# Attention with an adaptive layer norm and an MLP on one core: half cycles of three, three and two key tiles, and filling sums of 256 columns that share a bank

## The chip, the cores and the metric

One core of a Trainium2 chip runs the whole program. Its engines are TensorE (PE; its weight loads are listed apart as PEld), VectorE (DVE), ScalarE (ACT), GpSimd (POOL) and SyncE (SP, which here issues DMAs). The metric is device time in microseconds, the median over several executions. One execution was also profiled.

## The reference

An input x of 2048 rows and 512 columns goes through a transformer block whose layer norms are modulated by a condition vector c. The attention has 32 query heads of 16 columns and one key and one value head for all of them. The MLP is 1376 wide and its gelu is the tanh form.

```
mod = silu(c) @ w_mod                       # six rows of 512: sa, ca, ga, sb, cb, gb
h = layernorm(x) * (1 + ca) + sa
q, k, v = h @ wq, h @ wk, h @ wv            # q: 32 heads of 16; k and v: one head
p = softmax(q k^T / 4); o = p v
x = x + ga * (o @ wo)
h = layernorm(x) * (1 + cb) + sb
x = x + gb * (gelu(h @ w1 + b1) @ w2 + b2)
```

## The kernel before

**Units.** The 2048 rows are 8 blocks of 256 (`blocks`). A block has 8 units of 4 heads, so the loop at line 1350 goes through 64 units. In a unit, half s of the array (rows 0 to 63 or 64 to 127 of its contraction dimension) holds two heads j of 256 queries. There are 16 key tiles of 128 keys.

**What a unit does.** For each key tile and each half s a score product `e` (L607, 512 columns, 64 rows of the array) goes to one of three banks e0 to e2, and ScalarE writes its exponential to SBUF (L611, `p`). `pv` (L619, L628) multiplies the exponentials with the values: for each key tile four products of 32 array columns, which run at the same time and are listed as 8 instructions. The softmax's maximum is found ahead of time: 32 products `m` a unit (L505, 512 columns, 64 rows, tag `m` with three banks), each reduced by VectorE (`tensor_reduce`, L510). `put_max` (L529) takes the last maximum of a unit, turns it on VectorE and GpSimd and sends it by DMA into a row of the query tile, where the score product subtracts it. `lead` sets how far the maxima run ahead (32 a unit).

**Filling.** While one half of the array makes maxima and scores, the other works on a *batch* of other products, the filling: query projections of later blocks (`qproj_late`), and for each finished block its output projection, layer norm, transposes and MLP (`rest_steps`). A matrix product is three products of float32r parts (high and low). These jobs are Python generators in `queue`; `batches` (L167) cuts a sum into lists of products, `take` (L1169) fetches the next one, and `advance` goes on with the generator, which then also issues what reads the sum. A batch runs twice: rows 0 to 63 of its operands in one half cycle, rows 64 to 127 in the next, into the same bank, tag `x`. `half` (L187) lets the first product of a batch wait for the exponential of a score product (`state["witness"]`) that ran behind the other half's products, so that the two halves never write the bank at once.

**A cycle.** The loop at L1351 takes K and K+1, two pairs of key tiles X and Y: four cycles a unit. A cycle is:

1. `due()`, then a half cycle: half 1 gets n/2 = 4 maxima and 3 scores in turn (`mixture`, `beside`), half 0 the batch (6 products of 512 columns, or 12 of 256, `halves`) and a closing score (`follow`).
2. `end_step(*behind)`: the value products of the Y pair of the cycle before.
3. The other half cycle with the halves exchanged, the batch's second part in half 1, then what reads its sum.
4. `end_step(u, X)`: the value products of X.

`issue` (L1320) merges the two lists into program order: each entry has a length, and the list that stands earlier goes next. A maximum or score counts 1 and a product of a batch 0.75 for 512 columns (`AHEAD` / products), so that the batch stands somewhat ahead in program order. `beside` keeps the exponential of its last score back until the closing score's has been issued. Where the batch ends a sum, the reductions of the third and fourth maximum are issued behind what reads the sum (`hold`). Short batches (four products: the transposes, the last query groups) have an order of their own (`short`), and cycles without a batch another (`plain`), in which both halves share maxima and scores.

**Time in ticks.** `clock` counts four ticks a cycle, and `later(n, fn)` issues fn n ticks on (`due`). The DMAs that fetch a finished block's heads, the steps of the layer norm and of the gelu are placed so. For each of the 11 tiles of the first MLP `gelu` (L940) takes the sum out on VectorE with the bias (L949), squares it on ScalarE a tick later (L953), applies tanh four ticks later (L958), and GpSimd does the rest and splits the result into parts `gH` and `gL` six ticks later. The second MLP's sums are 512 columns wide, 33 products, and wait in Python until the gelu tiles they read have been issued (`made`).

**The end.** The last block's rest runs after the loop by itself on the whole array (`fast`), with what is left of the block before it (`tick`).

Of the kernel before, what the change touches and what calls it, by code (L numbers as in the profile page):

```python
# [32 lines left out]
BUSY = 5  # L33
BATCH = 6
SHORT = 4
LONG = (3, 1)
# [5 lines left out]
AHEAD = 4.5  # L42
# [8 lines left out]
def adaln_mqa_mlp(  # L51
# [127 lines left out]
    def whole(batch):  # L179
        for ps, a, b_, first_, last_ in batch:  # L180
            nc.tensor.matmul(ps, a, b_, start=first_, stop=last_)  # L181
# [5 lines left out]
    def half(one, s, behind=None):  # L187

        ps, a, b_, first_, last_ = one
        rows = slice(64 * s, 64 * s + 64)  # L190
        ins = nc.tensor.matmul(ps, a[rows], b_[rows], start=first_ and s == 0, stop=last_ and s == 1)  # L191
        if behind is not None:
            wait_for(ins, behind, "the other half of the array adds to the same bank")
# [254 lines left out]
    def qproj_late(b, g):  # L448
        ps = psum.tile([P, BQ], F32, name=f"qps{b}_{g}", tag="x")
        size_ = BATCH if (b, g) < LONG else SHORT  # L450
        yield from batches(ps, qpairs(b, g), size_)
        q32 = wts_pool["rest"].tile([P, BQ], F32, name=f"q32_{b}_{g}", tag="ot", bufs=2)
        if size_ == SHORT:
            nc.scalar.copy(q32, ps)
        else:
            nc.vector.tensor_copy(out=q32, in_=ps)
        qH, qL = qtiles(b, g)
        split(qH, qL, q32, nc.gpsimd, nc.gpsimd)
        later(4, lambda: send_q(b, g, qH, qL))
# [20 lines left out]
    class Max:  # L480
# [17 lines left out]
        def step(self, s, hold=None, **place):  # L498
# [4 lines left out]
            m = psum.tile([P, 512], F32, name=f"m{u}_{j}_{t}_{kc}_{s}", **(place or dict(tag="m", bufs=3)))  # L503
# [86 lines left out]
    def sexp(u, K, j, s, line=None):  # L590

        w = blocks[units[u][0]][1]
        qst = qsts[u]
        assert u in placed
        n = u * steps[0] + K
        if n < 3 and n not in pbufs:
            pbufs[n] = att.tile([P, 2, 2, 512], F32, name=f"p{n}", tag="p", bufs=3)
        pt = pbufs[n % 3]
        bank = banks.pop(0)
        banks.append(bank)  # L600
        e = psum.tile([P, 512], F32, name=f"e{u}_{K}_{j}_{s}", tag=f"e{bank}", bufs=1)
        rows = slice(64 * s, 64 * s + 64)
        if w == 512:
            kt, rhs = K, qst[rows, j, :]
        else:
            kt, rhs = 2 * K + j, qst[rows].rearrange("p j n -> p (j n)")
        nc.tensor.matmul(e, ks[rows, kt * P:(kt + 1) * P], rhs, start=True, stop=True)  # L607
        dst = pt[:, j, s, :]

        def exp():  # L610
            ins = nc.scalar.activation(dst, e, AF.Exp, scale=0.25)  # L611
            for old in written.pop((n - 3, j, s), ()):
                tc.declare_no_dep(ins.ins, old, reason="the products that read the tile's last contents come between the two")
            written.setdefault((n, j, s), []).append(ins.ins.name)
            return ins

        return exp() if line is None else line.append(exp)

    def pv(u, K):  # L619
        w = blocks[units[u][0]][1]  # L620
        if K == 0:
            accs[u] = psum.tile([P, w], F32, name=f"acc{u}", tag="v")
        pt = pbufs[(u * steps[0] + K) % 3]
        for kt in ([K] if w == 512 else [2 * K, 2 * K + 1]):
            for cidx in range(4):
                s, j = divmod(cidx, 2)
                rhs = pt[:, j, s, :] if w == 512 else pt[:, kt - 2 * K, s, j * w:(j + 1) * w]
                ins = nc.tensor.matmul(accs[u][32 * cidx:32 * cidx + 32, :], va[:, kt, :], rhs,  # L628
                                       start=kt == 0, stop=kt == NKT - 1)
                if kt % 2 and cidx:  # L630
                    wait_early(ins)

# [168 lines left out]
    def stir(starts):  # L801

        ps = psum.tile([P, BQ], F32, name=f"stir{len(idles)}", tag="x")
# [4 lines left out]
    def rest_steps(b, fast, rp, bank, ons, ready):  # L808
# [4 lines left out]
        for hf in range(w // HQ):  # L813
# [43 lines left out]
            pss = []  # L857
            for t in range(2):
                ps = psum.tile([P, D], F32, name=f"wops{b}_{hf}_{t}", **bank())
                pss.append(ps)  # L860
                if fast:
                    yield from batches(ps, out_pairs(t, range(KD - 1)), BATCH, end=False)
                    continue
                yield from batches(ps, out_pairs(t, range(KD)), BATCH)
                add_x(t, ps)

                for h in range(2):
                    later(3 - 2 * t + 2 * h, lambda t=t, h=h: stats(t, h))
            if fast:
# [10 lines left out]
            if not fast:  # L880
                later(4, lambda: rstd(0, 2))
                later(5, lambda: xhat(0))
                later(5, lambda: xhat(1))
                later(9, lambda: add_bias(0))
                later(9, lambda: add_bias(1))

                later(BUSY, lambda: state.update(busy=True))
                yield 8
# [3 lines left out]
            def modulate(dp, ps):  # L892
                if not fast:
                    src = rp.tile([P, 2, HQ], F32, name=f"tc{b}_{hf}_{dp}", tag="ot", bufs=2)
                    nc.scalar.copy(src, ps)
# [29 lines left out]
            else:  # L925
                for dp in range(KD // 2):
                    ps = psum.tile([P, 2, HQ], F32, name=f"tp2_{b}_{hf}_{dp}", **bank())
                    yield [(ps[:, d2, t * P:(t + 1) * P], xh[:, t, (2 * dp + d2) * P:(2 * dp + d2 + 1) * P], ident,
                            t + d2 == 0, t + d2 == 2) for t in range(2) for d2 in range(2)]
                    modulate(dp, ps)  # L930
                whole_h = clock[0] + 4
                state.update(busy=False, turns=2)
# [7 lines left out]
            def gelu(f, ps):  # L940
# [7 lines left out]
                else:  # L948
                    nc.vector.tensor_scalar(out=z, in0=ps, scalar1=b1c[:, f:f + 1], scalar2=None, op0=ALU.add)  # L949
# [20 lines left out]
                later(5 if fast else 6, last)  # L970
# [12 lines left out]
            for f in range(GROUP if fast else 0, NF):  # L983
# [3 lines left out]
                ps = psum.tile([P, HQ], F32, name=f"w1ps{b}_{hf}_{f}", **bank())  # L987
                pairs = [(w1t[:, 0, k, :], w1t[:, 1, k, :], hH[:, k, :], hL[:, k, :]) for k in range(KD)]
                if f or fast:
                    yield from batches(ps, pairs, 2 * BATCH)  # L990
                else:

                    yield from batches(ps, pairs, BATCH, lambda k: k < KD // 2 or clock[0] >= whole_h)
                if fast:
                    later(1, lambda f=f, ps=ps: gelu(f, ps))
                    yield 2
                else:
                    gelu(f, ps)
                    if f + 3 < NF:
                        later(1, lambda f=f: fetch_w1(b, w1ts, f + 3))  # L1000
            stage[b] = 1

            def store(t, ps, cols=slice(0, D)):
                row = row0 + hf * HQ + t * P
                ot = rp.tile([P, D], F32, name=f"ot{b}_{hf}_{t}", tag="ot", bufs=2)
                nc.vector.tensor_tensor(out=ot[:, cols], in0=ps[:, :cols.stop - cols.start], in1=x1[:, t, cols], op=ALU.add)
                send = lambda: nc.sync.dma_start(out=of[row:row + P, cols], in_=ot[:, cols])
                if fast:
                    send()
                else:  # L1010
                    later(2, send)
# [3 lines left out]
            for t in range(2):  # L1015
                sl = slice(t * P, (t + 1) * P)
                for cols in (slice(0, D), ):
                    place = dict(tag="m", bufs=3) if b == len(blocks) - 2 and t else bank()
                    ps = psum.tile([P, D], F32, name=f"w2ps{b}_{hf}_{t}_{cols.start}", **place)
# [480 lines left out]
```

## Time and profile before

| | us |
|---|---|
| median of 3 runs | 1565.02 (1564.38 to 1565.74) |
| profiled execution, first to last instruction | 1563.1 |
| TensorE busy | 1546.5 (99%) |
| VectorE busy | 1401.7 (90%) |
| ScalarE busy | 1228.8 (79%) |
| GpSimd busy | 681.7 (44%) |

The page gives the profiled execution by its span, the time from its first to its last instruction; the device times of the runs lie some 1.9 us above it. In the rows below, a line of the timeline has the start in us from the span's start, the length, the engine, the line of the code, the operation, what it writes and reads, and how many were merged into one row (their length then covers all). A bracket gives the engine's idle time before the row and what ended it. A line of a group has, behind the count, the busy time of all and the mean of one in ns, then the engine's idle time before them. A line of the windows has the stretch, its length, and for PE, PEld, DVE, ACT and POOL the busy us and the instruction count, then the clock, the share of DMA and GB/s. The granted clock was 1.00 throughout.

### The profile page before, as it was taken

Reading aid. Unit: us, or ns where it says so; the run is one execution under the profiler, and the core shown is the slowest. Engines: PE = TensorE matmul, PEld = TensorE weight load, DVE = VectorE, ACT = ScalarE, POOL = GpSimd, SP = SyncE. Lnnn points to the kernel's source line nnn. Section 1 sums busy time; section 2 is a strip of 40 time slices with the busy share of each in tenths; the row PEclk is TensorE's granted clock in tenths of the full one; section 3 lists DMA queues with packets and bytes.
Section 4 is the critical chain, followed back from the end, with each engine's and each line's share of the span. In section 5 each row is a group of like instructions: output and inputs, shape, how many; then the busy total and the mean of one; then the engine's idle time right before and its main releaser. Section 6 shows DMA issues by size and latency. Waiting matters only on the chain.

```text
span 1563.1 us, 41433 instructions
## 1 busy us (share of the span) xinstructions
PE 1546.5 (99%) x16387; PEld 959.9 (61%) x16387; DVE 1401.7 (90%) x2479; ACT 1228.8 (79%) x2392; POOL 681.7 (44%) x1194
## 2 busy tenths in 40 slices
PE   7999999999999999999999999999999999999999
PEld 4455555567655665557655675556655676556667
DVE  7999999999999999999999999999999999999625
ACT  5577778788777887788877887788877888788853
POOL 5545433877323570246422472245611573235711
PEclk9999999999999999999999999999999999999999
DMA  7235412313030211213022120303112130312241
GB/s 244 97 96 194 152 52 89 120 52 97 19 110 19 83 60 35 93 29 99 29 62 69 57 84 26 105 16 97 43 50 79 46 97 20 102 34 66 81 150 61
DMA packets 83126, 121.63 MB, mean 78 GB/s; under 512 B 19614, under 2 KB 56222, under 8 KB 82676
## 3 DMA queue, kind: packets, MB, share of 16 engines
q1 hardware_dynamic: 82916, 118.97, 23.5%
q8 instruction: 130, 2.13, 0.6%
q14 instruction: 64, 0.52, 0.1%
q10 hardware_dynamic: 16, 0.00, 0.0%
HBM read 91.13 MB, written 27.27 MB: 76 GB/s over the span
## 4 chain that ended last, share of the span: by engine, by line
PE 84%; DVE 10%; issue 3%; POOL 2%; DMA 1%; ACT 0%; ACTq 0%; SPq 0%; POOLq 0%; DVEq 0%
PE acc L628 28%; PE m L505 24%; PE e L607 16%; DVE mx L510 8%; PE w1ps L191 8%; PE w2ps L181 2%; PE w2ps L191 1%; PE w1ps L181 1%; DMA xt<-in_A_x_dram 1%; PE qps L191 1%; PE tp L191 1%; PE wops L191 1%; PE kps L162 1%; DVE st L835 1%; DVE x L828 1%
## 5 line engine op out<-in xcount | busy, mean ns | idle before, releaser
L510 DVE TENSOR_REDUCE mx<-m 128x1 f32<-128x512 f32 x2048 | 1270.5, 682 | 86.9 <-PE m L505 63.8
L611 ACT ACTIVATE p<-e 128x512 f32<-128x512 f32 x2048 | 1099.3, 598 | 257.4 <-PE e L607 110.5
L505 PE MATMUL m<-ks,qst 64*128 64x512 f32 x2048 | 832.4, 429 | 1.9 <-DVE mx L510 0.6
L607 PE MATMUL e<-qst,ks 64*128 64x512 f32 x2048 | 747.6, 412 | 0.1
L628 PE MATMUL acc<-p,va 128*32 128x256 f32 x8192 | 548.0, 385 | 0.0
L505 PEld LDWEIGHTS m<-ks,qst 64*128 64x128 f32 x2048 | 366.5, 184 | 212.3 <-DVE mx L510 174.8
L607 PEld LDWEIGHTS e<-qst,ks 64*128 64x128 f32 x2048 | 362.5, 184 | 95.2 <-ACT p L611 71.1
L628 PEld LDWEIGHTS acc<-p,va 128*32 128x32 f32 x8192 | 213.7, 109 | 213.1 <-issue 110.0
L553 POOL TENSOR_SCALAR mt<-turned 8x32 f32<-8x32 f32 x256 | 53.1, 208 | 418.9 <-DVE turned L559 406.9
L191 PE MATMUL w1ps<-h2H,w1t 64*128 64x256 f32 x1232 | 235.6, 287 | 0.0
L191 PEld LDWEIGHTS w1ps<-h2H,w1t 64*128 64x128 f32 x1232 | 185.8, 184 | 28.9 <-DVE mx L510 17.7
L191 PE MATMUL w1ps<-h2L,w1t 64*128 64x256 f32 x616 | 169.2, 275 | 0.0
L191 PE MATMUL w2ps<-w2H,gH 64*128 64x512 f32 x284 | 123.8, 436 | 0.0
L191 PEld LDWEIGHTS w1ps<-h2L,w1t 64*128 64x128 f32 x616 | 114.0, 185 | 0.0
L191 PE MATMUL w2ps<-w2L,gH 64*128 64x512 f32 x282 | 110.9, 393 | 0.0
L191 PE MATMUL w2ps<-w2H,gL 64*128 64x512 f32 x282 | 110.2, 391 | 0.0
L954 POOL TENSOR_SCALAR tt<-tt 128x256 f32<-128x256 f32 x77 | 31.0, 403 | 142.6 <-ACT tt L953 109.3
L137 POOL TENSOR_TENSOR gL<-z,gH 128x256 fp32r<-128x256 f32 x77 | 57.0, 740 | 6.4
L955 POOL TENSOR_TENSOR tt<-tt,z 128x256 f32<-128x256 f32 x77 | 56.7, 736 | 6.4
L965 POOL TENSOR_TENSOR z<-tt,z 128x256 f32<-128x256 f32 x77 | 56.4, 733 | 6.0
L964 POOL TENSOR_TENSOR tt<-tt,z 128x256 f32<-128x256 f32 x77 | 56.4, 732 | 0.0
L191 PEld LDWEIGHTS w2ps<-w2H,gL 64*128 64x128 f32 x282 | 52.2, 185 | 0.4
(190 smaller groups left out, 1480.9 us busy)
## 6 DMA issues: line engine op xcount, KB each, us to landing
w1t<-dw SPq DMA_DIRECT2D x82, 512.0 KB
qst<-dq SPq DMA_DIRECT2D x384, 32.0 KB
do<-oc SPq DMA_DIRECT2D x64, 128.0 KB
dw<-w1s SPq DMA_DIRECT2D x11, 512.0 KB
xt<-in_A_x_dram SPq DMA_DIRECT2D x4, 1024.0 KB
dq<-qH SPq DMA_DIRECT2D x16, 256.0 KB
dq<-qL SPq DMA_DIRECT2D x16, 256.0 KB
x<-in_A_x_dram SPq DMA_DIRECT2D x8, 512.0 KB
```

The lines of the kernel that those rows point to most:

```text
L137: eng_l.tensor_tensor(out=dst_l, in0=src, in1=raw(dst_h), op=ALU.subtract)
L181: nc.tensor.matmul(ps, a, b_, start=first_, stop=last_)
L191: ins = nc.tensor.matmul(ps, a[rows], b_[rows], start=first_ and s == 0, stop=last_ and s == 1)
L505: nc.tensor.matmul(m, qsts[u][rows, j, t * P:(t + 1) * P], ks[rows, kc * 512:(kc + 1) * 512], start=True, stop=True)
L510: nc.vector.tensor_reduce(out=self.mx[u][:, i, kc:kc + 1], in_=m, axis=AX.X, op=ALU.max)
L553: nc.gpsimd.tensor_scalar(out=mt[:, g:g + 32], in0=turned[g:g + 4 * T, :], scalar1=1.0, scalar2=0.0, op0=ALU.mult, op1=ALU.add)
L607: nc.tensor.matmul(e, ks[rows, kt * P:(kt + 1) * P], rhs, start=True, stop=True)
L611: ins = nc.scalar.activation(dst, e, AF.Exp, scale=0.25)
L628: ins = nc.tensor.matmul(accs[u][32 * cidx:32 * cidx + 32, :], va[:, kt, :], rhs, start=kt == 0, stop=kt == NKT - 1)
L955: nc.gpsimd.tensor_tensor(out=tt, in0=tt, in1=z, op=ALU.mult)
L964: nc.gpsimd.tensor_tensor(out=tt, in0=tt, in1=z, op=ALU.mult)
L965: nc.gpsimd.tensor_tensor(out=z, in0=tt, in1=z, op=ALU.add)
```

## The change

The loop takes three cycles a unit in place of four. `GROUPS` gives each cycle's key tiles X and Y: 3 and 3, 2 and 3, 3 and 2. The maxima are shared out by key tiles, so a cycle of six has 12 and one of five has 10. The exponentials' SBUF room, 12 tiles of 512 columns as before, is handed out tile by tile (`free`, `slots`) instead of by pairs.

The filling's bank is now one tile `fill` for the whole loop (tag `x`). Its sums are 256 columns wide and take its two halves in turn; only the transposes take it whole (`wide`). So the sums of the query projection, the output projection and the second MLP become two each. `compose` puts a batch together, up to 16, 16 and 14 units of 256 columns in the three cycles (two more where that ends a sum), across the ends of sums and jobs. What reads a sum waits for the batch's last product (`reads`), and the first product of the next batch waits for the readers as well as for the witness. Since the start of a sum marks the whole bank to be overwritten, only the first sum of an empty bank is started; one that follows beside a running sum finds its half zeroed by ScalarE (`finish`).

The first MLP's sums are taken out, with the bias, by ScalarE instead of VectorE. The query sums are copied by ScalarE, in two halves. The additions that take out the output projection and the second MLP stay on VectorE, now 256 columns each. Several steps are placed at other ticks: the gelu's last step five ticks on instead of six, the layer norm's steps two ticks nearer to each other. A tick is a quarter of a cycle as before, and there are 12 in a unit instead of 16. A finished block's job goes to the front of the queue instead of its end. `short` is gone, and `AHEAD` 0.75 says the same share for a product as before.

```
-BUSY = 5
+BUSY = 3
-SHORT = 4
-LONG = (3, 1)
+GROUPS = ((3, 3), (2, 3), (3, 2))
+UNITS = (16, 16, 14)
+SPILL = 2
-AHEAD = 4.5
+AHEAD = 0.75
...
+        def place(self):
+            return fill["bank"] if self.wide else fill["bank"][:, 256 * self.where:256 * self.where + 256]
...
+    def reads(ins):
+        if fill["last"] is not None:
+            wait_for(ins, fill["last"], "the filling's bank is being written")
+        fill["reads"].append(ins)
+        return ins
...
-                    nc.vector.tensor_scalar(out=z, in0=ps, scalar1=b1c[:, f:f + 1], scalar2=None, op0=ALU.add)
+                    reads(nc.scalar.activation(z, ps, AF.Identity, bias=b1c[:, f:f + 1]))
...
-                later(5 if fast else 6, last)
+                later(5, last)
...
+    def compose(cap):
+        batch, ends, used = [], [], 0
+        while True:
+            if not pulled:
+                op = pull()
+                if op is None:
+                    break
+                pulled.append(op)
+            one, n = pulled[0]
+            left = sum(units_of(b_) for _, _, b_ in one.ops[n:])
+            if n == 0:
+                where = (0, 1) if one.wide else (fill["next"],)
+                if any(fill["unread"][r] for r in where) or used and used + SPILL >= cap:
+                    break
+                begin = not any(fill["flight"])
...
+            if used + units_of(one.ops[n][2]) > cap + (SPILL if used + left <= cap + SPILL else 0):
+                break
...
+        return batch, ends, used / 2
+
+    def finish(ends, ins):
+        fill["last"] = ins
+        for one in ends:
+            one.done(one)
...
+        for one in ends:
+            if not one.wide and fill["flight"][1 - one.where]:
+                fill["reads"].append(nc.scalar.copy(one.place(), zeros.to_broadcast([P, HQ])))
+                fill["zero"][one.where] = True
...
-        for K in range(0, steps[u], 2):
-            goal = lead[u] + (lead[u + 1] - lead[u]) * (K + 2) / steps[u]
+        kt = 0
+        for (nx, ny), room in zip(GROUPS, UNITS):
+            X, Y = list(range(kt, kt + nx)), list(range(kt + nx, kt + nx + ny))
+            kt += nx + ny
+            goal = lead[u] + (lead[u + 1] - lead[u]) * kt / NKT
...
-            batch = take() if behind else None
...
+            batch, ends, long = compose(room) if behind else ([], [], 0)
+            if batch:
+                k = min(max(1, round((n / 2 + nx + ny - long) / 2)), nx + ny - 1)
+                which = X + Y
+                groups = [mixture(maxes(1, n // 2, 0.01), beside(1, which[:-k])),
+                          exps(0, which[:k - 1]) + halves(batch, 0) + [(1.0, lambda: follow(0, which[k - 1]))]]
+                issue(*groups)
...
+                issue(mixture(maxes(0, n // 2, 0.01, hold), beside(0, which[k:])),
+                      exps(1, which[-k:-1]) + halves(batch, 1) + [(0.0, go_on), (1.0, lambda: follow(1, which[-1]))])
```

372 lines of the change are left out of this document (212 added, 160 removed).

## The prediction

> **What bounds the kernel now.** I read the page first (busy shares, the chain, the costliest groups), then the timeline of a few half cycles, then the groups and windows of the engines that the change loads.
>
> ```profile
> span 1563.1 us, 41433 instructions
> PE 1546.5 (99%) x16387; PEld 959.9 (61%) x16387; DVE 1401.7 (90%) x2479; ACT 1228.8 (79%) x2392; POOL 681.7 (44%) x1194
> PE 84%; DVE 10%; issue 3%; POOL 2%; DMA 1%; ACT 0%; ACTq 0%; SPq 0%; POOLq 0%; DVEq 0%
> L510 DVE TENSOR_REDUCE mx<-m 128x1 f32<-128x512 f32 x2048 | 1270.5, 682 | 86.9 <-PE m L505 63.8
> L611 ACT ACTIVATE p<-e 128x512 f32<-128x512 f32 x2048 | 1099.3, 598 | 257.4 <-PE e L607 110.5
> ```
>
> TensorE is busy 99% and carries 84% of the chain, but VectorE is at 90%: the second bound is close. The loop of 64 units has this frame:
>
> ```profile
> 79.59 0.49 PE L191 MATMUL qps<-h0H,wqH 64*128 64x512 f32 x1
> ...
> 1508.25 1.93 PE L628 MATMUL acc<-p,va 128*32 128x256 f32 x32
> ...
> 1510.11 0.50 PE L181 MATMUL wops<-woH,onH 128*128 128x512 f32 x1
> ```
>
> From 79.59 to 1510.11 the loop takes 1430.5 us: 510 of its 512 half cycles, 2.80 each. One full half cycle, array and VectorE:
>
> ```profile
> 999.91 0.49 PE L505 MATMUL m<-ks,qst 64*128 64x512 f32 x1
> 1000.25 0.39 PE L607 MATMUL e<-qst,ks 64*128 64x512 f32 x1
> 1000.44 2.48 DVE L510 TENSOR_REDUCE mx<-m 128x1 f32<-128x512 f32 x4 [0.36 <-PE m L505]
> 1000.48 0.39 PE L505 MATMUL m<-ks,qst 64*128 64x512 f32 x1
> ...
> 1001.41 0.41 PE L505 MATMUL m<-ks,qst 64*128 64x512 f32 x1
> ...
> 1001.75 1.07 PE L628 MATMUL acc<-p,va 128*32 128x256 f32 x16
> 1002.75 0.49 PE L505 MATMUL m<-ks,qst 64*128 64x512 f32 x1
> ```
>
> Seven 512-column products stand behind each other on each half of the array. I call such a place a slot. The second starts 0.34 after the first, the seventh at 1.50, so a slot is (1.50-0.34)/5 = 0.23 us. The value products begin 0.34 after the last slot's start, and the next half cycle 1.00 after that. A half cycle is 0.34 + 0.23 x (slots-2) + 0.34 + values, here 2.84. The values of two key tiles cost 1.00; the row at 1508.25 has four, and 1.86 pass until 1510.11, so a tile is 0.43 and the change of tiling costs 1.00-0.86 = 0.14, beside the 0.34 at either end of the slots. That is what fewer half cycles can save.
>
> **Part 1: six half cycles in place of eight.** A unit keeps its 64 half-array products for maxima and scores, its 16 value tiles (16 x 0.43 = 6.88) and nearly its filling: 16+16+14 = 46 pieces of 256 columns against 4 x 12 = 48. The code gives a half cycle 6 maxima and 4 scores beside 1 score, 16 pieces and 1 score (ten slots each) where it has three tiles on both sides; where five tiles are split in two, 5 maxima and 3 or 4 scores, and nine slots. By the array alone: ten slots 0.34+8x0.23+0.34 = 2.54 (with 0.232), nine 2.30; values 2 x 1.00 + 4 x 1.43 = 7.72. Unit: 2 x 2.54 + 4 x 2.30 + 7.72 = 22.0, against 8 x 2.84 = 22.7. The switching saved, 0.7 a unit, would be 46 us over 64 units.
>
> But the maxima have three banks, as before, and now come six in a row instead of four. The first reduction starts 0.53 behind its product (999.91 to 1000.44); four take 2.48, so they follow at (2.48-0.68)/3 = 0.60. The sixth product needs the third reduction's bank: 0.53 + 2x0.60 + 0.68 = 2.41. What such a wait looks like stands in a half cycle without filling:
>
> ```profile
> 1032.92 6.66 DVE L510 TENSOR_REDUCE mx<-m 128x1 f32<-128x512 f32 x11
> ...
> 1033.60 0.50 PE L607 MATMUL e<-qst,ks 64*128 64x512 f32 x2
> ...
> 1034.85 0.18 PEld L505 LDWEIGHTS m<-ks,qst 64*128 64x128 f32 x1 [0.41 <-DVE mx L510]
> ...
> 1035.28 1.07 PE L628 MATMUL acc<-p,va 128*32 128x256 f32 x16
> 1036.28 0.19 PEld L607 LDWEIGHTS e<-qst,ks 64*128 64x128 f32 x2 [0.41 <-ACT p L611]
> ```
>
> The third of the eleven reductions ends at 1032.92 + 2x0.598 + 0.68 = 1034.80; the waiting weights load at 1034.85, and the value products begin 0.43 later. So in the ten-slot half cycles the values begin at 2.41+0.05+0.43 = 2.89, not 2.54. With five maxima it is the second reduction: 1.81+0.05+0.43 = 2.29, level with the array's 2.30. In the kernel before it was the first: 1.21+0.48 = 1.69, inside 1.84. The six half cycles are 2.89+1.00, 2.89+1.43, 2.30+1.43, 2.30+1.00 and twice 2.30+1.43: 22.70 a unit. VectorE takes back 45 of the 46 us.
>
> A thinner batch does not shorten these, since maxima set them; only a cycle with no filling does.
>
> ```profile
> L181 PE MATMUL w2ps<-w2H,gL 128*128 128x512 f32 x35 | 13.9, 396 | 0.0
> ```
>
> The queue holds 14 query groups of 24 pieces and 7 blocks of 328 (48 output projection, 16 transposes, 132 and 132), less what is left for the end: now 35 products in each of three forms run there on the whole array, 22 of them the last block's, so about 38 in all of the block before it, or 76 pieces. 336+2296-76 = 2556 pieces of 64 x 46 = 2944. Some 25 of 192 cycles stay empty. An empty half cycle now lasts 2.68 (1033.60 to 1036.28), 0.16 under a full one; with the score banks as its limit I take 0.2: 25 x 2 x 0.2 = 10 us. Loop after: 64 x 22.70 - 10 = 1443; before, with the two half cycles left out, 1430.5+5.7 = 1436. Term: **+7**.
>
> **Part 2: sums of 256 columns.** Twice the weight loads and products for the same columns. The first MLP has them already:
>
> ```profile
> 1072.11 0.38 PE L191 MATMUL w1ps<-h2H,w1t 64*128 64x256 f32 x1
> 1072.33 0.28 PE L191 MATMUL w1ps<-h2H,w1t 64*128 64x256 f32 x1
> 1072.44 0.39 PE L607 MATMUL e<-qst,ks 64*128 64x512 f32 x1
> 1072.45 0.27 PE L191 MATMUL w1ps<-h2L,w1t 64*128 64x256 f32 x1
> 1072.56 0.27 PE L191 MATMUL w1ps<-h2H,w1t 64*128 64x256 f32 x1
> ...
> 1074.95 0.18 PEld L505 LDWEIGHTS m<-ks,qst 64*128 64x128 f32 x1 [0.41 <-DVE mx L510]
> ```
>
> One each 0.115, half a slot, and the half cycle is 2.84 as with 512. Price nothing; the loads hide behind the other piece's streaming.
>
> **Part 3: ScalarE takes the first MLP's sums, and clears banks.** A sum that ends while its neighbour runs is zeroed by a ScalarE copy.
>
> ```profile
> 675.00:1075.00 400.00, 399.79 (x4496) 249.98 (x4496) 375.45 (x655) 328.59 (x644) 169.54 (x316) 1.00 0.19 60
> L949 DVE TENSOR_SCALAR z<-w1ps,b1c 128x256 f32<-128x256 f32 x77 | 37.1, 482 | 3.8 <-PE w1ps L191 3.5 <-PE m L505 0.3
> L945 ACT ACTIVATE z<-w1ps,b1c 128x256 f32<-128x256 f32 x11 | 5.2, 474 | 3.0 <-PE w1ps L181 3.0
> L640 ACT COPY oc<-acc 128x256 f32<-128x256 f32 x64 | 23.8, 372 | 5.8 <-PE acc L628 5.6
> L953 ACT ACTIVATE tt<-z 128x256 f32<-128x256 f32 x77 | 32.4, 421 | 0.0
> 1044.94 2.06 ACT L611 ACTIVATE p<-e 128x512 f32<-128x512 f32 x4 [0.15 <-PE e L607]
> ```
>
> VectorE loses 77 x 0.48 = 37 us, worth nothing on the path where 2.84 did not contain it. ScalarE gains, for each sum, 0.47 (L945) and 0.37 for the clearing (no such row; the nearest, the 256-column copy of L640). In the first MLP's stage, 77 x 12/46 = 20 units, 3.83 sums a unit come with two gelu steps of 0.42: 3.83 x 1.68 = 6.4 us beside 32 exponentials. Back to back these follow at (2.06-0.60)/3 = 0.49, 15.7 in all, so 22.1 of 22.7. Lower bound of the cost: 0, since that fits. Upper: with the exponentials at the row's 1099.3/64 = 17.2, 6.4+17.2+0.4 = 24.0, 1.3 a unit, 26 us. I worked through the shortest half cycle (2.30+1.00 = 3.30): first exponential at about 0.77, five of them 2.45, then 1.33 sums' worth of evacuation, clearing and square, 1.33 x 1.27 = 1.7 by durations, about 1.3 back to back: done at 4.5 to 4.9, where the next half's first exponential could start at 3.30+0.53 = 3.83. The fourth score waits for that exponential's bank, so 0.55 to 1.1 a unit are lost, one half cycle in six. I take 0.6 x 20 = **+12**.
>
> **Part 4: VectorE's evacuations.** The second MLP's and output projection's additions become twice as many at about 0.48 (L949, the nearest 256-column row). One in the 3.30 us half cycle, behind five reductions (0.53+3.00), ends at 4.0 where the next reduction could start at 3.83, and more with the unit's final maximum. Between 0 (absorbed) and 0.5 for the third of 56 sums that fall there, 9 us; I take **+5**. Late GpSimd products for the second MLP, whose first sum now runs in two cycles: 0 to 3 us a block, 0 to 21; I take 0, since the gelu steps were also moved a tick earlier. The end keeps its left-over work: 0, plus or minus 8.
>
> **Sum.** 1563.1 + 7 + 12 + 5 = 1587.1; the runs lie 1.9 above the profiled span (1565.02 in the median), so **1589 us**.
>
> **Rivals.** *The array is the bound after all* (faster): if the maxima's reductions keep ahead, the ten-slot half cycles start their values at 2.54, and 128 x 0.35 = 45 us come off. With ScalarE and VectorE hidden too: 1565 + 7 - 45 + 5 (empty cycles save less) = 1532. For it: in full half cycles VectorE now never holds the array. Against: 2.41 follows from two rows. It decides at a stall of 0.30 per ten-slot half cycle if nothing else costs, at 0.16 if all the other terms hold.
>
> *Strict order on the array.* The filling stands ahead of its place in program order (0.375 for half a slot), so the closing score is issued before the last two scores or maxima of the other half. If a product cannot start before an earlier one, five-tile half cycles of 0 + 16 + 1 (two a unit) last a slot longer: 0.23 x 2 x 64 x 0.87 = 26 us, 1615. Against: the piece at 1072.33 starts ahead of the score at 1072.44, which the code issues before it. The Trainium skill's page "TensorE: Matmul & The Clock Gate", section "The mechanism", states the strict form (starts and ends in program order); by that rule the sum would be 1615, and the trace disagrees by one place at least.
>
> *ScalarE or GpSimd sets the first MLP's stage:* the upper ends, 26+21 in place of 12: 1624.
>
> *The cycles even out:* empty cycles and fewer switches cancel the new waits, 1565.
>
> **How the numbers follow.** The forecast (1570 to 1605) 0.45; strict order or its like 0.12; ScalarE or GpSimd 0.14; the array's bound, wholly or partly, 0.24; even 0.05. The range leaves out the lower half of the faster cases and the end of the slow ones: 1545 to 1630. Runs of this kernel differ by 0.1%, so 0.2%, 3 us, is about what can be told from no change. Faster 0.24, same 0.05, slower 0.71.
>
> **What would show it.** In the trace after: value products of 24 starting 2.89 behind the half cycle's start where there are six maxima, with a weights load of m waiting for VectorE; 2.30 at five; pieces of 256 at 0.115; ScalarE nearly without idle time in the first MLP. Wrong if ten-slot half cycles take 2.54, or if first-half filling waits for clearing copies everywhere.

## The result, and the profile after

The changed kernel takes 1755.26 us in the median (1752.56 to 1768.16) where the kernel before, run beside it, takes 1564.78: a ratio of 1.123, with an interval of 1.120 to 1.127. Slower was forecast, but at 1589 us, and the time lies far outside the range to 1630.

The page after, first its span, busy times and chain, then the two costliest groups:

```profile
span 1753.6 us, 44436 instructions
...
PE 1641.2 (94%) x17936; PEld 1125.2 (64%) x17936; DVE 1380.2 (79%) x2419; ACT 1271.5 (73%) x2564; POOL 682.5 (39%) x1194
...
PE 84%; ACT 5%; DVE 5%; SPq 2%; DMA 2%; issue 1%; POOL 1%; DVEq 0%; POOLq 0%
...
L547 DVE TENSOR_REDUCE mx<-m 128x1 f32<-128x512 f32 x2016 | 1259.0, 684 | 278.9 <-PE m L542 156.9
L647 ACT ACTIVATE p<-e 128x512 f32<-128x512 f32 x2048 | 1087.6, 600 | 358.6 <-PE e L644 323.8
```

TensorE is no longer the bound throughout: 94% in place of 99%, so 112 us of its span are idle (16.6 before). Its share of the chain is 84% as before; ScalarE has 5% of it (0 before) and VectorE 5% (10 before). Yet no engine has become full instead: VectorE fell from 90 to 79%. It waited 278.9 us ahead of its reductions (86.9 before), ScalarE 358.6 ahead of the exponentials (257.4). Engines that wait for each other suggest a problem of order, which the page alone does not show.

Windows of the loop, of the end, and of short stretches in which the array waits (the columns as in the section on the profile before):

```profile
85.00:1693.00 1608.00, 1517.52 (x17282) 1041.35 (x17278) 1283.92 (x2216) 1207.43 (x2440) 631.55 (x1118) 0.97 0.20 64
1693.00:1753.00 60.00, 52.05 (x330) 45.61 (x323) 27.45 (x71) 15.95 (x41) 5.33 (x6) 0.97 0.26 97
488.60:500.50 11.90, 6.69 (x48) 4.70 (x44) 3.93 (x6) 3.48 (x6) 3.96 (x3) 0.71 0.05 12
493.07:499.90 6.83, 5.60 (x35) 4.41 (x39) 2.63 (x4) 2.98 (x6) 0.00 (x0) 0.50 0.00 1
544.27:547.68 3.41, 2.16 (x20) 1.00 (x20) 3.41 (x9) 2.69 (x6) 2.32 (x3) 1.00 0.00 0
549.10:556.20 7.10, 6.28 (x40) 2.58 (x38) 3.77 (x6) 3.65 (x7) 3.84 (x3) 0.50 0.18 50
```

The loop lasts 1608 us in place of 1430.5, which is +178 of the +190.5 between the two profiled spans. The start is 5 us longer and the end 7. The last four rows show something that the loop before has nowhere: stretches in which the array is granted half of its clock. The 0.71 of the third row is a mean: from 493.07 to 499.90 the clock was 0.50.

Three kinds of half cycle show where the loop's time is. The first is one that begins a unit, once in each block (start us, length, engine, line, operation):

```profile
478.99 0.44 POOL L138 TENSOR_TENSOR ml<-mt,mh 8x128 fp32r<-8x128 f32 x1
...
481.82 0.33 SPq L780 DMA_DIRECT2D drs<-rsum  x1
...
483.29 2.47 SPq L797 DMA_DIRECT2D os<-drs  x4
...
485.85 1.88 SPq L513 DMA_DIRECT2D qst<-dq  x3
...
491.24 0.67 SPq L585 DMA_DIRECT2D qst<-mh  x1
...
493.80 0.76 PE L644 MATMUL e<-qst,ks 64*128 64x512 f32 x1 [4.71 <-DMA qst<-ml]
```

The parts of the unit's maximum row are ready on GpSimd at 479.43. SyncE's queue sends them from 491.24 only: ahead of them stand a finished block's factors on their way to DRAM and back (L780, L797) and the next query tile (L513). The score that reads the row waits 4.71 us, and the pieces behind it then run at 0.50 of the clock. The half cycle takes 11.9 us instead of 3.9. Seven of them come to 9.9 to 11.9.

The second is the ordinary half cycle of nine slots, 16 pieces and values of three tiles, which starts at 707.35:

```profile
709.22 0.27 PE L193 MATMUL fill<-w2H,gL 64*128 64x256 f32 x1
709.25 0.50 PE L644 MATMUL e<-qst,ks 64*128 64x512 f32 x2
709.59 0.39 PE L542 MATMUL m<-ks,qst 64*128 64x512 f32 x1
709.91 1.50 PE L662 MATMUL acc<-p,va 128*32 128x256 f32 x24
```

The last piece starts at 709.22, 1.87 behind the start, as the array allows. But a score and the last maximum of the *other* half of the array start only then: the score at 709.25, beside the closing score (709.33; they share one row), and the maximum another 0.34 later. The values begin at 2.56 where 2.30 was forecast. The median over 79 such half cycles is 3.99 (forecast 3.73), and 3.56 over the 39 with values of two tiles (3.30). The ten-slot ones have 4.04 and 4.39 (3.89 and 4.32), those of nine slots with 14 pieces 3.75 (3.73).

The third has no filling:

```profile
343.51 0.50 PE L644 MATMUL e<-qst,ks 64*128 64x512 f32 x2
...
344.69 0.50 PE L644 MATMUL e<-qst,ks 64*128 64x512 f32 x1 [0.45 <-ACT p L647]
...
346.60 0.49 PE L542 MATMUL m<-ks,qst 64*128 64x512 f32 x1 [0.80 <-DVE mx L547]
...
347.03 1.07 PE L662 MATMUL acc<-p,va 128*32 128x256 f32 x16
```

A score waits for an exponential, a maximum for a reduction, and the values begin 3.52 behind the start. The loop has 30 of this kind: 24 last from 4.5 to 7.1 us and six, which have fewer maxima, 3.0 to 3.6, where I had taken them to be 0.2 shorter than the full ones.

### The profile page after: what moved, and what is told of

Same layout as the page of the kernel before. It is cut to its first block, busy times and chain, and to the rows that moved or that the text cites. A ratio compares the mean times of both kernels' runs of the same rounds, so it can differ in the third digit from the quotient of the medians.

```text
span 1753.6 us, 44436 instructions
## 1 busy us (share of the span) xinstructions
PE 1641.2 (94%) x17936; PEld 1125.2 (64%) x17936; DVE 1380.2 (79%) x2419; ACT 1271.5 (73%) x2564; POOL 682.5 (39%) x1194
## 4 chain that ended last, share of the span: by engine, by line
PE 84%; ACT 5%; DVE 5%; SPq 2%; DMA 2%; issue 1%; POOL 1%; DVEq 0%; POOLq 0%
PE acc L662 27%; PE m L542 20%; PE fill L193 18%; PE e L644 15%; DVE mx L547 4%; ACT p L647 3%; SPq L585 1%; DMA qst<-ml 1%; PE w2ps L182 1%; PE w1ps L182 1%; DMA xt<-in_A_x_dram 1%; SPq L513 1%; PE fill L182 1%; PE kps L163 1%; ACT tt L1005 0%
## 5 line engine op out<-in xcount | busy, mean ns | idle before, releaser
L547 DVE TENSOR_REDUCE mx<-m 128x1 f32<-128x512 f32 x2016 | 1259.0, 684 | 278.9 <-PE m L542 156.9
L647 ACT ACTIVATE p<-e 128x512 f32<-128x512 f32 x2048 | 1087.6, 600 | 358.6 <-PE e L644 323.8
L193 PE MATMUL fill<-h2H,w1t 64*128 64x256 f32 x1232 | 233.6, 284 | 0.0
L193 PEld LDWEIGHTS fill<-h2H,w1t 64*128 64x128 f32 x1232 | 190.0, 186 | 0.1
L193 PE MATMUL fill<-h2L,w1t 64*128 64x256 f32 x616 | 173.1, 281 | 0.0
L193 PE MATMUL fill<-w2H,gH 64*128 64x256 f32 x560 | 164.0, 293 | 0.0
L193 PE MATMUL fill<-w2H,gL 64*128 64x256 f32 x560 | 162.4, 290 | 0.0
L193 PE MATMUL fill<-w2L,gH 64*128 64x256 f32 x558 | 158.4, 284 | 0.0
L193 PEld LDWEIGHTS fill<-h2L,w1t 64*128 64x128 f32 x616 | 114.7, 186 | 0.2 <-ACT p L647 0.2
L193 PEld LDWEIGHTS fill<-w2H,gL 64*128 64x128 f32 x560 | 107.4, 192 | 0.4
L193 PEld LDWEIGHTS fill<-w2H,gH 64*128 64x128 f32 x560 | 107.5, 192 | 0.0
L193 PEld LDWEIGHTS fill<-w2L,gH 64*128 64x128 f32 x558 | 106.8, 191 | 0.0
```

The costliest lines, as they stand in the source:

```text
L547: nc.vector.tensor_reduce(out=self.mx[u][:, i, kc:kc + 1], in_=m, axis=AX.X, op=ALU.max)
L647: ins = nc.scalar.activation(slot(i), e, AF.Exp, scale=0.25)
```

## The experiments

Half cycles are named below by their slots and pieces; lengths are medians, counted from one start to the next. Every time stands beside the kernel before on the same chip (1564.0 to 1566.0).

### The late row, and the filling's lead

```
-MAX_WAIT = (1, 4)
+MAX_WAIT = (1, 2)
```

> The changed kernel with the four transfers of a unit's maximum row issued two ticks after the maximum instead of four, so that they stand ahead of the next query loads on SyncE's queue. Late-row theory: once a block the first half cycle of a unit stands 7 us because these transfers wait behind 4 + 8 others; with them ahead, eight stalls of about 7 us go, 57 us in all: 1755 to about 1698, and the granted clock comes back from 0.97 to near 1.00. Rival (the stall is the query load itself or GpSimd, and the row is only what the profile names last): less than 10 us.

1718.7 us (two executions, 1714.5 and 1722.9): 36.5 less than the changed kernel, not 57. The changed kernel's list of waits (us in total, times, longest) has this line, and this run's has not:

```profile
PE e L644 <- DMA qst<-ml: 41.2, 20, 4.7
```

At least part of the missing 20 us moved to the next transfer in the same queue. From this run's list:

```profile
PE m L542 <- DMA qst<-dz: 11.4, 7, 2.7
```

Maxima now wait for the next query tile, 11.4 us in 7 times. The half cycles that begin a unit still reach 5.2 to 7.0.

```
-AHEAD = 0.75
+AHEAD = 1.0
```

> The changed kernel with AHEAD 1.0 instead of 0.75, so that a filling piece counts its full half slot in the merge and the closing score stands behind the other half's products in program order. Order theory: the nine-slot half cycles lose their extra 0.24 us, 203 of them, 47 us: 1755 to about 1708; the value products begin 2.30 to 2.35 behind the half cycle's start instead of 2.56. Rival (ScalarE's clearing copies delay the witness, and with it the pieces): no more than 10 us either way, and 2.56 stays.

1776.8 us: 21 *more*. The 16-piece half cycles of nine slots did get shorter, by 0.13, but those of 14 pieces went from 3.75 to 4.10, because a piece now stands behind a score that waits. The expectation took the lead for a cost alone; it also protects the pieces.

> Both edits. If the two theories hold and do not share their time: 57 + 47 = 104 us, 1755 to about 1651. What then stays above the kernel before (1565) would be the maxima's three banks (ten-slot half cycles 2.89 instead of 2.54), the half cycles without filling or with little, and the ends. If one frees time that the other eats: 1680 to 1700.

1726.4 us (1722.4 to 1730.4), far from 1651, and no better than the early row alone.

### The same lead in the kernel before

```
-AHEAD = 4.5
+AHEAD = 6.0
```

> The kernel before with the filling standing at its own place in program order (AHEAD 6.0 for six products in place of 4.5), so that the closing score is issued behind the other half's last product and no piece ahead of its time. If the array's program order binds products of one half behind waiting products of the other, a piece now stands behind a score or maximum that waits for its bank: half cycles of 2.84 grow by 0.1 to 0.3, +50 to +130 us over some 430 of them. If the order does not matter: 1565, within 3.

1580.8 us, ratio 1.0097 (1.0082 to 1.0112). So the program's order on TensorE is worth time in the kernel before too, but less than expected: mainly the 138 half cycles of the first MLP grew, by 0.08 in the mean, and those of six 512-column products kept their 2.84.

### Do the reductions hold the array?

```
-  in_=m, axis=AX.X, op=ALU.max
+  in_=m[:, 0:256], axis=AX.X, op=ALU.max
```

> Both edits, and each reduction of a maximum reads 256 of its 512 columns (and the exponential's scale is made small so that nothing overflows): the output is not the reference's, since half of each maximum and the softmax's scale are left out; instructions and their order stay. Bank theory: the third of six reductions then ends by about 1.8 instead of 2.41, so ten-slot half cycles begin their values at 2.54 instead of 2.89 or later: 94 x 0.36 = 34 us or a little more under the run with both edits. Rival (the array's slots or ScalarE's exponentials set these half cycles): under 10 us.

1657.7 us, 69 less than with both edits above. That looked like VectorE as the cause, in twice the size expected. The control:

> The kernel before, whose reductions read 256 of the 512 columns (half of each maximum left out, and the softmax's scale changed so that the exponentials stay finite). The control for the halved reductions. If the full half cycles before are bound by the array, as predicted (2.84), these stay at 2.84 and only the half cycles without filling (2.68 each) can shorten: 1565, at the least 1535. If VectorE set part of the time before as it does after (-69 us there), about 1500.

1553.4 us: 12 us less. The full half cycles stayed at 2.84 and only thin ones changed (2.71 to 2.65), so the kernel before is bound by its array, as the prediction had it.

### The filling by itself, and ScalarE's part

```
-GROUPS = ((3, 3), (2, 3), (3, 2))
-UNITS = (16, 16, 14)
+GROUPS = ((2, 2), (2, 2), (2, 2), (2, 2))
+UNITS = (12, 12, 12, 12)
```

> The changed kernel with the key tiles shared out as before (four cycles of 2 and 2, 12 units of filling each); sums of 256 columns, batches across sums, the clearing copies and ScalarE's evacuations all stay. Theory (the half cycles of five and six tiles, and what a unit of 12 ticks does to the maximum row, carry the loss): about 1565, within 20. Rival (the filling's bank, its clearing copies and ScalarE carry a large part): 1620 or more.

1605.8 us, ratio 1.026 (1.025 to 1.028), between the two. So about 150 us belong to the new half cycles, with what their fewer ticks do to SyncE's queue, and about 41 to the new filling. Its trace shows ScalarE in the first MLP, and what starts the next half cycle's filling:

```profile
550.77 0.48 ACT L996 ACTIVATE z<-fill,b1c 128x256 f32<-128x256 f32 x1
...
551.28 0.38 ACT L1285 COPY fill<-mm 128x256 f32<-128x256 f32 x1
551.59 1.08 ACT L647 ACTIVATE p<-e 128x512 f32<-128x512 f32 x2
...
551.88 0.18 PEld L542 LDWEIGHTS m<-ks,qst 64*128 64x128 f32 x1 [0.41 <-DVE mx L547]
...
552.24 0.18 PEld L193 LDWEIGHTS fill<-h2H,w1t 64*128 64x128 f32 x1 [0.17 <-ACT p L647]
```

The evacuation (`z`) and the clearing copy stand ahead of two exponentials. The half cycle starts at 551.88, but its first piece at 552.24, when an exponential of the half cycle before is done. That half cycle takes 3.15 us; some 90 are between 3.1 and 3.35.

> The kernel before with one line changed: the first MLP's sums go out through ScalarE. Step of the prediction: ScalarE's work in that stage, without clearing copies, is 3.83 x (0.47 + 2 x 0.42) = 5.0 us beside 15.7 of 22.7 us a unit, so it fits: 0 to +5, and less idle time of ScalarE there. Rival (ScalarE's place in the order of a half cycle costs, as in the 3.30 us half cycle of the prediction): +10 to +26.

1565.4 us, ratio 1.000 (0.999 to 1.001): the evacuation through ScalarE costs nothing by itself.

```
-  fill["reads"].append(nc.scalar.copy(one.place(), zeros...))
+  fill["reads"].append(nc.vector.tensor_copy(out=one.place(), in_=zeros...))
```

> The previous kernel with the old half cycles and the new filling (1605.8), whose 91 clearing copies of the filling's bank go through VectorE in place of ScalarE. Its trace has 90 half cycles of the first MLP at 3.15 in place of 2.85: the copy (0.38) stands on ScalarE ahead of the exponentials, so the closing score's exponential comes late and the next batch's first piece waits for it. If that is the cause: 90 x 0.30 = 27 us less, 1579. Rival (the evacuation through ScalarE alone, or the wait for the readers, is what holds the batch): 1600 or more.

1605.9 us: no change, and my expectation fell. VectorE's rows of the same place:

```profile
551.63 0.43 DVE L1285 COPY fill<-mm 128x256 f32<-128x256 f32 x1 [0.42 <-ACT z L996]
551.97 3.67 DVE L547 TENSOR_REDUCE mx<-m 128x1 f32<-128x512 f32 x6
```

Here the copy waits for `z` and the next half cycle's reductions wait behind the copy. The pieces start with the half cycle, and the maxima are late instead.

> The kernel with the old half cycles and the new filling (1605.8), without the 91 clearing copies (so sums that start beside a running one add to the old content: the clearing is left out). If the copy lies on the path on either engine: 1575 to 1580, the 90 half cycles of 3.15 back at 2.85. If the batches across sums or the 256-column evacuations are what costs: 1600 or more.

1584.3 us: without the copies 21.5 us are gone, so the copy lay on the path on either engine. It explains about half of the 41. The other 20 stay open; 15 half cycles of 3.3 to 3.5 and 28 more full batches than before are part of them.

> The changed kernel with the maximum row sent two ticks earlier (1718.7 alone), and the 70 clearing copies through VectorE. In these half cycles of nine and ten slots VectorE sets the values' start and the batch's first piece mostly starts with the half cycle, so ScalarE's copies lie beside other work: 0 to -8, 1711 to 1719. If the copies cost here what they do in half cycles of two tiles: -21, 1698. If VectorE's 0.3 us each lengthen its chain: +10 or more.

1712.9 us, but from 1705.7 to 1720.0, against 1718.7: unclear. Nor does this run price the copies here: with the old half cycles the same move to VectorE changed nothing either, while leaving the copies out was worth 21.5 us. The changed kernel was not run without them.

### The rest of the queue

```
-  nc.sync.dma_start(out=drs[b]..., in_=rsum)
+  nc.gpsimd.dma_start(out=drs[b]..., in_=rsum)
-  nc.sync.dma_start(out=oss[hf][:, 1, g, :], in_=src)
+  nc.gpsimd.dma_start(out=oss[hf][:, 1, g, :], in_=src)
```

> The changed kernel with the maximum row sent two ticks earlier (1718.7), and a finished block's softmax factors (their way to DRAM and back, L780 and L797) issued from GpSimd's queue in place of SyncE's. Theory (SyncE's queue stands still behind these transfers, and the next query tile, issued behind them, comes late: the eight half cycles that begin a unit at 5.2 to 7.0 us): these fall to about 4.1, 15 to 20 us less, about 1700. Rival (the transfers are late for another reason, or GpSimd, waiting for the round trip, is late with its own steps): within 5 of 1718, or slower.

1701.9 us (1700.0 to 1704.7), as expected: 16.8 less than the early row alone, whose two executions lie 8 us apart. The maxima's wait for the query tile fell to one of 3.2 us:

```profile
PE m L542 <- DMA qst<-dz: 3.2, 1, 3.2
```

One half cycle that begins a unit stays at 9.0, the last block's.

### The order on the array

```
+  a = 1.0 if nx + ny == 5 and len(batch) == 16 else AHEAD
```

> The changed kernel with the maximum row sent two ticks earlier (1718.7), and the filling no longer ahead in program order only where five maxima stand beside 16 pieces. Order theory: these 118 half cycles fall from 4.00 and 3.56 by the 0.13 that the run without any lead showed, while the others keep their lengths: 15 us less, about 1703. If that run's 0.13 came from its other half cycles' lengths: no change.

1713.9 us, 5 less than the 1718.7 and not 15, which is within the spread of that run's two executions. The 118 half cycles did fall by the 0.13 in the median, to 3.86 and 3.42, and summed over both profiles they are 11 us shorter. Those of 14 pieces took 8 of it back (3.77 to 3.98 in the mean): 13 of them have a score that waits for ScalarE's exponential. Of the 38 with ten slots and values of two, 12 rose from 4.04 to about 4.37, but their sum grew by less than 2.

> The changed kernel with the maximum row sent early and the factors on GpSimd's queue (1701.9), whose reductions read 256 of the 512 columns (half of each maximum left out, and the softmax's scale changed so that the exponentials stay finite). If VectorE's reductions carry the rest: the half cycles fall to the array's lengths, 3.54 and 3.97 with ten slots and 3.30 and 3.73 with nine: 1560 to 1590. If the array's order carries as much: nine slots stay near 3.8 and ten near 3.9 and 4.2, about 1635.

1665.4 us, above both expected cases. The full half cycles with 16 pieces did not move at all: 3.99, 3.56, 4.04 and 4.56, the same as in the run with whole reductions. A nine-slot one of this kernel, which starts at 504.22:

```profile
506.10 0.28 PE L193 MATMUL fill<-woH,onL 64*128 64x256 f32 x1
506.13 0.49 PE L644 MATMUL e<-qst,ks 64*128 64x512 f32 x2
506.46 0.38 PE L542 MATMUL m<-ks,qst 64*128 64x512 f32 x1
506.78 1.50 PE L662 MATMUL acc<-p,va 128*32 128x256 f32 x24
```

The last piece, the two scores and the maximum stand as they did in the changed kernel. What the 36 us came from is mostly half cycles without filling (4.96 to 4.43; 22 us) and others with little. So neither VectorE nor the maxima's banks set the length of the full half cycles. The program's order is what is left. This is the end of a ten-slot half cycle in the changed kernel's list of TensorE's instructions, in program order:

```
L193 fill
L193 fill
L644 e33_1_0      the closing score, behind the last piece on its half
L542 m35_0_0_0    \ two maxima of the other half,
L542 m35_0_0_1    / issued behind the closing score
L662 acc ...
```

The list says how many come behind the closing score: with 16 pieces at 0.375 it stands at 6.0 in nine slots and at 7.0 in ten, and the other half's last two products at 6.01 and 7.01, or 7.01 and 8.01 (the first maximum counts 0.01). With 14 pieces none comes behind it, with 18 one, and in the kernel before one (4.5 against 5.01). Among those of 14, 16 and 18 pieces that the forecast covers, the ones that came out as forecast are those with none or one.

```
-AHEAD = 0.75
+AHEAD = 0.755
```

> The changed kernel with both transfers early (1701.9) and AHEAD 0.755 in place of 0.75: with 16 pieces the closing score is issued behind one more product of the other half, so that one and not two come after it. Order theory: nine slots 3.99 to 3.73 and 3.56 to 3.30 (118 x 0.26), ten slots 4.04 to 3.89 and 4.56 to 4.32, where the maxima's banks take over (38 x 0.15 and 38 x 0.24): 46 us less, 1656; up to 1675 if VectorE, with its reductions closer together, gives some back as in the run with nine slots in order. If the order is not the cause, a change of 0.005 does nothing: 1702.

1681.8 us, 20 less. The lengths are those of the order theory, and of the prediction: nine slots 3.76 and 3.33 (forecast 3.73 and 3.30), ten slots 3.90 and 4.34 (forecast 3.89 and 4.32). A nine-slot half cycle of this kernel, which starts at 691.26:

```profile
692.99 0.40 PE L644 MATMUL e<-qst,ks 64*128 64x512 f32 x1
...
693.13 0.28 PE L193 MATMUL fill<-w2H,gL 64*128 64x256 f32 x1
693.22 0.44 PE L542 MATMUL m<-ks,qst 64*128 64x512 f32 x1
693.25 0.41 PE L644 MATMUL e<-qst,ks 64*128 64x512 f32 x1
693.59 1.50 PE L662 MATMUL acc<-p,va 128*32 128x256 f32 x24
```

The score at 692.99 and the maximum at 693.22 now run beside the pieces, and the values begin at 2.33. The time gained is less than 46 us for two reasons that the trace shows: 20 of the 79 nine-slot half cycles with values of three stay at 4.0 to 4.2, which nothing here explains, and the 14-piece half cycles rose from 3.77 to 3.96 in the mean. In 13 of these a score waits for an exponential, as in this one, which starts at 484.27:

```profile
485.16 0.50 PE L644 MATMUL e<-qst,ks 64*128 64x512 f32 x1 [0.38 <-ACT p L647]
```

It is ScalarE that takes this back, and not VectorE, which the expectation named: with halved reductions, in the next run, the mean is still 3.95. The edit also moves one other place, in the middle of the merge: the ninth of 16 pieces stood at 3.0, ahead of a product of the other half at 3.01, and now stands at 3.02, behind it.

> The same with reductions that read 256 of the 512 columns (1665.4 with AHEAD 0.75; half of each maximum left out, softmax scale changed). Order theory: nine slots 3.73 and 3.30 as above, ten slots now to the array's 3.54 to 3.6 and 3.97 to 4.1: 118 x 0.26 + 38 x 0.45 + 38 x 0.5 = 67 us less, about 1600. If the order is not the cause: 1665.

1625.8 us, 40 less than the same kernel with AHEAD 0.75, and not 67. Ten slots fall to 3.63 and 4.13: with the order mended, the reductions do hold them, by 0.2 to 0.27.

> The changed kernel itself (1755.3) with AHEAD 0.755 and nothing else. Order theory: 40 us less, 1715, the late rows left as they are. Else 1755.

1741.6 us, 14 less than the changed kernel. The direction is that of the order. A third of the size came through. The late row's half cycles stay as they were. Summed over the two profiles, the nine slots with 16 pieces are 21 us shorter and the ten slots with 16 another 5; the half cycles of 14 and 17 pieces are 9 longer, and the loop starts 4 us later.

## Why the prediction was wrong

**The half cycles of nine slots, "and nine 2.30"** (Part 1, "by the array alone"). This step failed. It counted slots on each half of the array and took the halves to be independent. They share one program order: a product of one half that is issued behind a waiting product of the other half comes after it. The traces show that one product may stand behind it at no cost, and that the second starts late and with its weights not yet loaded. My rival "strict order" had the place right (half cycles of 0 + 16 + 1) and priced it at 26 us; 118 x 0.26 is 31. I gave it 0.12, because a piece at 1072.33 started ahead of a score that had been issued before it. The row is true, but it shows an overtaking by one product, and I read it as the absence of order. The Trainium skill, "TensorE: Matmul & The Clock Gate", section "The mechanism", lets products start and end only in program order; the traces agree with it to within one product (709.25 is ahead of the closing score at 709.33), and by that rule alone, 1615, I would have come nearer, but not near.

**"2.41+0.05+0.43 = 2.89"**, the maxima's banks in the ten-slot half cycles. The mechanism is there, but in the changed kernel something else lay over it. Ten slots with values of two, from 722.45 in the changed kernel and from 705.93 with AHEAD 0.755:

```profile
724.56 0.27 PE L193 MATMUL fill<-woH,onH 64*128 64x256 f32 x1
724.68 0.47 PE L644 MATMUL e<-qst,ks 64*128 64x512 f32 x1
724.86 0.70 PE L542 MATMUL m<-ks,qst 64*128 64x512 f32 x2
725.49 1.07 PE L662 MATMUL acc<-p,va 128*32 128x256 f32 x16
```

```profile
708.08 0.28 PE L193 MATMUL fill<-woH,onH 64*128 64x256 f32 x1
708.19 0.43 PE L644 MATMUL e<-qst,ks 64*128 64x512 f32 x1
708.40 0.50 PE L542 MATMUL m<-ks,qst 64*128 64x512 f32 x1
708.83 1.07 PE L662 MATMUL acc<-p,va 128*32 128x256 f32 x16
```

```profile
705.65 4.49 DVE L547 TENSOR_REDUCE mx<-m 128x1 f32<-128x512 f32 x7
```

In the first, two maxima follow the closing score and the values begin at 3.04; they did so with halved reductions too. In the second, one maximum is left, at 2.47, and the values begin at 2.90. There the banks decide, since halving the reductions brings 2.63. VectorE's row shows seven reductions without a pause across the half cycle: it is the bound of these half cycles once the order isn't. That the changed kernel's 4.39 lay near the forecast 4.32 was no confirmation.

**"An empty half cycle ... I take 0.2" less.** Wrong in sign. With six maxima and six scores, both halves taking turns, each kind runs into its three banks in program order (the rows from 343.51), and the 30 half cycles of that kind took 1.2 us more in the mean than I had forecast for a full one: 42 us more in all than the forecast allows for them. The one at 549.05, at half clock, took 7.1.

**What the prediction did not have at all: SyncE's queue.** I costed the ticks of the gelu and the norm, and not that a unit of 12 ticks in place of 16 puts a finished block's transfers, the next query tile and the maximum row into the same stretch of one queue. The two edits for it were worth 36.5 and 16.8 us, the largest single term. The late score also let the clock fall (0.50 from 493.07), so the price of such a wait is more than its length: the half cycle lost 8.0 us, and 4.71 of them are the row's wait. That the clock falls to one half after an idle window of about 3.4 us is stated by the Trainium skill, "TensorE: Matmul & The Clock Gate", section "Part 1: The HAM clock gate"; the trace agrees at 493.07, when the score of 493.80 had waited for 4.0 us, and on the size, 0.50. At 547.68 the clock fell as well, though the array had been busy for 2.16 of the 3.41 us before: there the measurement goes further than the rule.

**Part 2, nothing for the 256-column sums.** Right for the pieces themselves: in the half cycle from 707.35 the last ones start at 708.98, 709.10 and 709.22, 0.12 apart, where 0.115 was forecast. Whether the batches across sums cost nothing is not shown; they may be part of the 20 us that stay open in the run with the old half cycles.

**Part 3, +12 for ScalarE.** The sum is of the right size by accident. The evacuation costs 0 (0.999 to 1.001). The clearing copies cost 21.5 in half cycles of two tiles. I had priced them together with the evacuation and the square, through the bank of the fourth score; in the trace the batch's first piece waits behind them for an exponential. What they cost in the changed kernel's half cycles no run shows.

**Part 4, +5 for VectorE's additions, and 0 for late GpSimd products.** Not measured apart.

**The sum.** From 1755: the two transfers 53, one place in program order 20 (40 with halved reductions), the reductions in what is then left 56 (12 in the kernel before). 1626 remains, 72 above the kernel before with halved reductions.

The traces give the shares by kind of half cycle, against the forecast lengths (3.30 and 3.73, 3.89 and 4.32, 3.58 without filling). The changed kernel's half cycles are 173 us too long in all: 59 of them in nine that stand still for 3 us or more, seven of which begin a unit; 42 in the 30 without filling; 33 in nine slots with 16 pieces; 13 in ten slots with 16; 10 in ten slots with six; 16 in the others. So the step on the nine slots is the third in size, behind the queue, which had no term, and the empty half cycles, whose term had the wrong sign. In the last version (1626), against the array's lengths (3.54 and 3.97 for ten slots), 83 us stand over: 19 in ten slots with 16 pieces, 13 without filling, 12 in ten slots with six, 11 in nine slots with 16, 8 in those of 14, and 20 in the others. How much of this is the clearing copies stays open. None of the changed kernel's versions beats the kernel before.

## What to carry to other kernels

Where two halves of an array work side by side from one instruction stream, count not only each half's slots but the products that stand behind each other's waits in program order: here one was free and a second was not, and a change of 0.005 in an interleaving weight was worth 20 us. A length that comes out as forecast can have another cause; halving the suspected operation tells. When a cycle gets fewer, longer steps, list everything that a queue must issue between two steps, since a wait for it may also cost the clock.

## What was not expected of the hardware

One product overtakes a product of the other half by about 0.1 us (709.25 against the closing score at 709.33), never seen by two in the half cycles looked at. A product that could not load its weights ahead starts 0.31 to 0.34 behind the one before it, in place of 0.23. The granted clock fell to 0.50 behind a wait of 4.71 us, and also at 547.68, behind 3.41 us in which the array was listed as busy for 2.16 and no single wait was longer than 0.80: short waits in a row were enough there.
